# Inner loops in TensorE's program, and a first jump behind the unit loops, in a cached-attention decode kernel

## The chip, the cores and the metric

One core of a Trainium2 chip. The metric is the device time of one execution in microseconds (us). The kernel before was run three times: 1280.09 us in the median, 1279.94 to 1280.13.

## The reference: one decode step of attention and a gated layer

Four sequences (B), one new token each, 32 heads of 128, a cache of 8192 keys and values per head, all in bf16:

```python
h  = x + A(layernorm(x))
h2 = h + Bm(layernorm(h))
# A:  q = x @ wq, per head
#     p = softmax(einsum("bhqd,bhkd->bhqk", q, k_cache) * 128 ** -0.5)
#     A = einsum("bhqk,bhkd->bhqd", p, v_cache) @ wo
# Bm: (sigmoid(x @ w_gate) * (x @ w_up)) @ w_down
```

The two caches are 4 x 32 x 8192 x 128 elements each, 268 MB in bf16 each, and every element is used once. The weights (wq, wo, w_gate, w_up, w_down) make up some 14 MB more.

## The kernel before, in words

**Units.** The 128 pairs of sequence and head are taken four at a time: 32 units (`NU`). For one unit K is a load of 128 partitions by 64 KB (8.4 MB), and V another. Partition 32h + p holds 256 consecutive keys of head h.

**Slots and loads.** Three slots of 64 KB a partition lie in the tile KV: slots 0 and 1 for K of even and odd units, slot 2 for V (the last V goes to slot 0). SyncE (SP) issues all loads in one written-out order, wq first (L503), then k0, k1, v0, k2, v1, k3 and so on (L512). A K load waits until the transposes of the K in its slot are done (`t_kd`, a memset on VectorE, L342); a V load waits until the unit ahead of it has been weighted and summed (`t_vd`, the first product of L387). After the caches follow wo (L515) and w_gate (L517), w_up (L521), and three pieces of w_down (L526), each into a slot that came free. The output leaves by two small DMAs (L528).

**One unit** (`unit`). `k_chunk` runs 16 times: VectorE transposes 128 x 1024 words of K into one of two halves of kT (L327), and TensorE makes four products from it (L336), whose stationary operand is a window of the tile Lq, shifted by the number of the chunk. All 64 products of a unit sum into one PSUM bank, SBK; the first has `start`, the last `stop`. Then come the maxima (`maxima`, L343 to L348), the exponential on ScalarE (L350), the window of the next unit's query (`q_window`, L320), the weighting of V of the unit before (`pv`: 64 products of L377, the scaled copy L382 on ScalarE, four products of L387, which each run as two), and the transposed weights with their sum (`weights`, L356, L360).

**Order of work.** The class `_Prog` keeps one list of instructions for each engine, with the semaphore values that each waits for. `open`, `begin`, `end` and `close` turn a stretch that repeats into a hardware loop: the turns must be the same, and semaphores that belong to one engine are set back at each turn's end (`_rebase`, a semaphore instruction on L53). `play` (L110 to L118) writes the lists out; a loop's own edge has line L114. Unit 0 stands ahead of the loops. TensorE's loop has one unit a turn, 31 turns; that of VectorE and ScalarE has two units a turn, 15 turns, and the last unit stands behind it.

**Ends.** Ahead of the units, layer norm (L274 to L288), the query products from wq (L302) and their turning run. Behind them TensorE runs products that nobody reads, `filler` (L364: 36 ahead of the last `pv`, then 3, 10 and 4), the last `pv`, wo (L448), the second layer norm, gate and up (L467), down (L492), and VectorE adds the residual (L500).

Of the kernel before, what the change touches and what calls it, by code (L numbers as in the profile page):

```python
# [6 lines left out]
BF16 = mybir.dt.bfloat16  # L7
FP32 = mybir.dt.float32
ALU = mybir.AluOpType
ACT = mybir.ActivationFunctionType  # L10
AX = mybir.AxisListType


class _Prog:
    ENGS = ("sp", "act", "dve", "pool", "pe")

    def __init__(self, private):
        self.ops = {e: [] for e in self.ENGS}
# [4 lines left out]
        self.turn = {}  # L23
        self.turns = {}
        self.base = {}

    def token(self, key, by):
# [18 lines left out]
    def _rebase(self, eng):  # L46
        for key, owner in self.private.items():
            v = self.known[eng].get(key, 0)
            n = v - self.base.get(key, 0)
            if owner == eng and n:  # L50
                self.base[key] = v
                self._add(eng, ("rebase", key, n), lambda e, i, key=key, n=n:
                          e.wait_ge(self.sems[key], n).then_inc(self.sems[key], -n))  # L53

    def _add(self, eng, what, run):
        assert (eng in self.turn) == (eng in self.turns), eng
        if eng in self.turn:
            self.turn[eng].append((what, run))
        else:
            self.ops[eng].append(run)  # L60

    def _put(self, eng, todo, key, fn, incs, by):
        def run(e, i):
            for k, v in todo:
                e.wait_ge(self.sems[k], v)
            made = fn(e, i) if fn.__code__.co_argcount - len(fn.__defaults__ or ()) == 2 else fn(e)
# [6 lines left out]
        self._add(eng, (tuple(todo), key, incs), run)  # L73

    def emit(self, eng, fn, waits=(), incs=1, ch=None):
        todo = self._waits(eng, waits)
# [5 lines left out]
    def dma(self, eng, key, fn, waits=(), tok=None):  # L82
# [2 lines left out]
        self._put(eng, todo, key, fn, 1, 16)  # L85
        return tok

    def open(self, *engs):
        for e in engs:
            self._rebase(e)  # L90
            self.turns[e] = []

    def begin(self, *engs):
        for e in engs:
            self.turn[e] = []

    def end(self, *engs):
        for e in engs:
            self._rebase(e)
            self.turns[e].append(self.turn.pop(e))  # L100

    def close(self, *engs):
        for e in engs:
            first, *rest = self.turns.pop(e)
# [3 lines left out]
            self.ops[e].append((1 + len(rest), [m[1] for m in first]))  # L108

    def play(self, nc, name, e):  # L110
        for item in self.ops[name]:
            if isinstance(item, tuple):
                turns, runs = item
                with nc.Fori(0, turns, engines=OrderedEngineSet([e.engine])) as i:  # L114
                    for run in runs:
                        run(e, i)
            else:
                item(e, 0)  # L118


def bass_sequential_preLN__mha_block_cached__glu_gated_glu__decode_kernel(
# [13 lines left out]
    _, H, S, DH = A_k_cache.shape  # L135
# [6 lines left out]
    NU = B * H // HU  # L142
# [3 lines left out]
    TW = 1024  # L146
# [14 lines left out]
    with ExitStack() as es:  # L161
# [3 lines left out]
        def raw(t):  # L165
            return t.tensor if hasattr(t, "tensor") else t
# [146 lines left out]

        t_tr, t_sc, t_pv, t_ex, t_mx, t_exp, t_ptz, t_lq, t_ocp, t_rs, t_kd, t_vd, t_sum = ({} for _ in range(13))
        TU = 2

        def q_window(u, t=0):
            dst = bass.AP(raw(Lq), 15, [[528, 128], [128, 4], [16, 8]])
            msk = bass.AP(raw(mask), 0, [[8, 128], [0, 4], [1, 8]])
            t_lq[u] = emit("dve", lambda e, i: e.tensor_tensor(  # L320
                dst, bass.AP(raw(q_all), i * (4 * TU) + 4 * (u - TU * t), [[NU * 4, 128], [1, 4], [0, 8]]), msk, ALU.mult),
                           [t_q, t_lq0, t_mask, t_sc.get((u - 1, NT - 1))], ch="d2p")

        def k_chunk(u, c):
            o = slots["k", u] * (SLOT // 2) + c * TW
            w = [toks["k", u], t_sc.get((u, c - 2)) if c >= 2 else t_sc.get((u - 1, NT - 2 + c)), t_sum.get(u - 1) if c == 1 else None]
            t_tr[u, c] = emit("dve", lambda e: e.transpose(  # L327
                kT[:, (c % 2) * TW:(c % 2 + 1) * TW], KVw[:, o:o + TW]), w, ch="d2p")

            def f(e):  # L330
                ins = None
                for t in range(4):
                    hb, par = t // 2, t % 2
                    rhs = bass.AP(kTb.tensor, kTb.offset + (c % 2) * 2 * TW + hb * 64 + par,
                                  [[kTb.ap[0][0], 128], [128, 16], [2, 32]])
                    ins = e.matmul(bank[SBK], Lq[:, 128 * t + 15 - c:128 * t + 143 - c], rhs,  # L336
                                   start=(c == 0 and t == 0), stop=(c == NT - 1 and t == 3))
# [25 lines left out]
        def filler(n):  # L363
            emit("pe", lambda e: [e.matmul(bank[XS], Lq[:, 0:128], Lq[:, 0:512], start=True, stop=True) for _ in range(n)][-1],  # L364
                 [t_ps0, t_lq[NU - 1]], incs=0)

        def pv(u, t):
            t_rs[u] = emit("dve", lambda e: e.reciprocal(rsb[:, :], bank[QB[1]][:, 1:2]), [t_sum[u]], ch="d2a")  # L368
            slot = slots["v", u]
            ob = 512 * OBK  # L370

            def f(e, ks):
                made = []
                for k in ks:
                    j, n, r4 = k % 4, k // 4, k % 4
                    lhsT = PTz[:, 512 * r4 + n:512 * r4 + n + 481:32]
                    made.append(e.matmul(PS[32 * j:32 * j + 16, ob:ob + 512], lhsT,  # L377
                                         KV[:, slot * SLOT + 512 * k:slot * SLOT + 512 * (k + 1)],
                                         start=(k < 4), stop=(k >= 60), tile_position=(0, 32 * j)))
# [4 lines left out]
            def fs(e, i, qs):  # L384
                ins = None
                for q in qs:
                    ins = e.matmul(bass.AP(raw(PS), i * 4 + (512 * EX + 4 * (u - t)), [[4096, 128], [1, 4]]),  # L387
                                   O_sb[:, 128 * q:128 * (q + 1)], lane[:, q:q + 13:4],
                                   start=False, stop=(u == NU - 1 and q == 3), skip_group_check=True)
                return ins  # L390
            t_vd[u] = emit("pe", lambda e, i: fs(e, i, (0,)), [t_ocp[u], t_selc, t_ps0], ch="p2x")
            t_ex[u] = emit("pe", lambda e, i: fs(e, i, (1, 2, 3)), ch="p2d")

        def unit(u, t=0):
            for c in range(NT):
                k_chunk(u, c)
# [183 lines left out]
```

## Time and profile before

| what | value |
|---|---|
| median of three runs | 1280.09 us (1279.94 to 1280.13) |
| span of the profiled execution | 1278.5 us |
| the execution's own time beside the span | not recorded by itself; the median is 1.6 us longer than the span |
| instructions | 10886 |
| HBM read | 550.77 MB, 431 GB/s over the span |
| PE, DVE, ACT busy | 782.6, 759.6, 58.8 us |
| L336, the score products | x2048, 421 ns mean |
| L327, the transposes of K | x512, 1229 ns mean |

The span runs from the first to the last instruction of one profiled execution. PE is TensorE's products, PEld its weight loads, DVE VectorE, ACT ScalarE, POOL GpSimd, SP SyncE. "Busy" leaves out register, branch, semaphore and DMA-issuing instructions. [...]

### The profile page before, as it was taken

To read this page: it belongs to the slowest core of one execution; us is meant where nothing else is said; L and a number is where in the kernel's file an instruction comes from. 1 tells how busy PE (TensorE), PEld (TensorE's weight loads), DVE (VectorE), ACT (ScalarE), POOL (GpSimd) and SP (SyncE) were. 2 spreads that over 40 slices of the span, in tenths; PEclk is the share of its full clock that TensorE was granted. 3 is DMA by queue.
4 is the path that set the end of the run, shared out by engine and by line. 5 is a ranking of instruction groups with operands and counts; after the bars stand their busy time and mean duration, and the time that the engine had idled before them with its cause. 6 is when DMAs were issued, how large, how long until landed. Compare 5 with 4: busy or idle time off the path is not lost. (4 is left out here: it accounts for less than half of the span.)

```text
span 1278.5 us, 10886 instructions
## 1 busy us (share of the span) xinstructions
PE 782.6 (61%) x4609; PEld 292.2 (23%) x4609; DVE 759.6 (59%) x917; ACT 58.8 (5%) x114; POOL 5.7 (0%) x22
## 2 busy tenths in 40 slices
PE   1666765557755557755567655567655577555578
PEld 0222222222212222212222212222222222122223
DVE  1876765556665557665567655566655566655571
ACT  2000000000000000000000000000000000000001
POOL 1000000000000000000000000000000000000000
PEclk8888877788877788777788877788777888777889
DMA  9999999999999999999999999999999999999998
GB/s 425 425 427 431 437 443 426 431 429 445 435 429 429 435 443 431 429 431 439 441 426 431 429 445 435 429 429 435 443 431 429 431 441 439 426 431 429 443 437 343
DMA packets 10252, 550.83 MB, mean 431 GB/s; under 512 B 1148, under 2 KB 1160, under 8 KB 1416
## 3 DMA queue, kind: packets, MB, share of 16 engines
q1 hardware_dynamic: 10232, 550.77, 99.6%
q8 instruction: 3, 0.05, 0.0%
q10 hardware_dynamic: 16, 0.01, 0.0%
q14 instruction: 1, 0.01, 0.0%
HBM read 550.77 MB, written 0.00 MB: 431 GB/s over the span
## 5 line engine op out<-in xcount | busy, mean ns | idle before, releaser
L336 PE MATMUL PS<-kT,Lq 128*128 128x512 bf16 x2048 | 590.0, 421 | 347.2 <-DVE kT L327 329.5
L327 DVE STREAM_TRANSPOSE kT<-KV 128x1024 f32<-128x1024 f32 x512 | 611.7, 1229 | 307.9 <-DMA KV<-in_A_k_cache_dram 259.0
L336 PEld LDWEIGHTS PS<-kT,Lq 128*128 128x128 bf16 x2048 | 177.5, 104 | 746.7 <-DVE kT L327 581.4
L356 DVE STREAM_TRANSPOSE PTz<-E_sb 32x512 bf16<-32x512 bf16 x128 | 89.9, 703 | 128.9 <-PE PS L387 125.2
L377 PE MATMUL PS<-KV,PTz 128*16 128x512 bf16 x2048 | 116.9, 381 | 0.0
L360 PE MATMUL PS<-part,headw 128*128 128x2 f32 x64 | 17.8, 348 | 100.4 <-DVE PTz L356 100.4
L350 ACT ACTIVATE E_sb<-PS,negm 128x512 bf16<-128x512 f32 x32 | 22.0, 687 | 1141.3 <-DVE negm L348 1141.3
L377 PEld LDWEIGHTS PS<-KV,PTz 128*16 128x16 bf16 x2048 | 59.0, 110 | 56.0 <-issue 13.6
L387 PE MATMUL PS<-lane,kT 128*128 128x4 f32 x256 | 33.6, 255 | 30.8 <-ACT kT L382 30.8
L343 DVE TENSOR_REDUCE part<-PS 128x1 f32<-128x512 f32 x32 | 22.1, 692 | 35.9 <-PE PS L336 35.9
L387 PEld LDWEIGHTS PS<-lane,kT 128*128 128x128 f32 x256 | 31.0, 191 | 46.1 <-issue 44.7
L360 PEld LDWEIGHTS PS<-part,headw 128*128 128x128 f32 x64 | 15.1, 293 | 103.7 <-DVE PTz L356 103.7
L382 ACT ACTIVATE kT<-PS,rsb 128x512 f32<-128x512 f32 x32 | 22.0, 687 | 64.5 <-PE PS L377 64.5
L364 PE MATMUL PS<-Lq 128*128 128x512 bf16 x53 | 15.1, 447 | 0.1
L427 DVE TENSOR_TENSOR kT<-PS,mask 128x512 bf16<-128x512 f32 x1 | 0.7, 692 | 16.3 <-PE PS L387 16.3
L320 DVE TENSOR_TENSOR Lq<-q_all,mask 128x32 bf16<-128x32 bf16 x32 | 9.5, 298 | 0.0
L364 PEld LDWEIGHTS PS<-Lq 128*128 128x128 bf16 x53 | 5.6, 112 | 8.9 <-issue 5.3
L345 DVE STREAM_TRANSPOSE turn<-part 128x32 f32<-128x32 f32 x32 | 6.8, 212 | 1.1
L348 DVE STREAM_TRANSPOSE negm<-mxr 128x32 f32<-128x32 f32 x32 | 6.8, 211 | 1.1
L368 DVE RECIPROCAL rsb<-PS 128x1 f32<-128x1 f32 x32 | 6.3, 198 | 0.7 <-PE PS L360 0.7
L346 DVE TENSOR_SCALAR_CACHE_REDUCE turn<-turn 128x32 f32<-128x32 f32 x32 | 5.9, 186 | 1.1
L302 PE MATMUL PS<-KV,kT 128*4 128x512 bf16 x32 | 3.4, 594 | 5.1 <-DMA KV<-in_A_wq_dram 5.1
(65 smaller groups left out, 49.1 us busy)
## 6 DMA issues: line engine op xcount, KB each, us to landing
KV<-in_A_wq_dram SPq DMA_DIRECT2D x1, 4096.0 KB, 12.2
KV<-in_A_wo_dram SPq DMA_DIRECT2D x1, 4096.0 KB, 27.4
KV<-in_B_w_gate_dram SPq DMA_DIRECT2D x1, 1792.0 KB, 31.5
KV<-in_B_w_up_dram SPq DMA_DIRECT2D x1, 1792.0 KB, 35.3
KV<-in_B_w_down_dram SPq DMA_DIRECT2D x1, 1024.0 KB, 32.7
KV<-in_A_k_cache_dram SPq DMA_DIRECT2D x32, 50.3
KV<-in_A_v_cache_dram SPq DMA_DIRECT2D x32, 31.4
KV<-in_B_w_down_dram SPq DMA_DIRECT2D x1, 512.0 KB, 33.5
```

What stands on the lines that cost most here:

```text
L320: t_lq[u] = emit("dve", lambda e, i: e.tensor_tensor(dst, bass.AP(raw(q_all), i * (4 * TU) + 4 * (u - TU * t), [[NU * 4, 128], [1, 4], [0, ...
L327: t_tr[u, c] = emit("dve", lambda e: e.transpose(kT[:, (c % 2) * TW:(c % 2 + 1) * TW], KVw[:, o:o + TW]), w, ch="d2p")
L336: ins = e.matmul(bank[SBK], Lq[:, 128 * t + 15 - c:128 * t + 143 - c], rhs, start=(c == 0 and t == 0), stop=(c == NT - 1 and t == 3))
L343: a = emit("dve", lambda e: e.tensor_reduce(part[:, 0:1], bank[SBK], AX.X, ALU.max), [t_sc[u, NT - 1], t_pool], ch="d2d")
L345: a = emit("dve", lambda e: e.transpose(turn_[:, :], part[:, :]), [a], ch="d2d")
L350: t_exp[u] = emit("act", lambda e: e.activation(E_sb[:, :], bank[SBK], ACT.Exp, bias=negm[:, 0:1], scale=SCALE, accum_out=part[:, 1:2]), [ ...
L356: return [e.transpose(PTz[32 * q:32 * (q + 1), :].rearrange("p (r q c) -> p r q c", r=4, q=4)[:, :, q, :], E_sb[32 * q:32 * (q + 1), :].re ...
L360: t_sum[u] = emit("pe", lambda e: e.matmul(bank[QB[1]][:, 0:2], headw[:, :], part[:, 0:2], start=True, stop=True), [t_ptz[u], t_selc], ch= ...
L364: emit("pe", lambda e: [e.matmul(bank[XS], Lq[:, 0:128], Lq[:, 0:512], start=True, stop=True) for _ in range(n)][-1], [t_ps0, t_lq[NU - 1] ...
L377: made.append(e.matmul(PS[32 * j:32 * j + 16, ob:ob + 512], lhsT, KV[:, slot * SLOT + 512 * k:slot * SLOT + 512 * (k + 1)], start=(k < 4), ...
L382: t_ocp[u] = emit("act", lambda e: e.activation(O_sb, bank[OBK], ACT.Copy, scale=rsb[:, 0:1]), [t_pv[u], t_rs[u]], ch="a2p")
L387: ins = e.matmul(bass.AP(raw(PS), i * 4 + (512 * EX + 4 * (u - t)), [[4096, 128], [1, 4]]), O_sb[:, 128 * q:128 * (q + 1)], lane[:, q:q + ...
```

## The change

Three things are edited, and the class `_Prog` is extended to write nested loops.

First, the scores: a unit's 64 products become one clearing product with a weight tile of bf16 words and a moving operand of zeros (`clear`, with `start`), and a loop of 8 turns on TensorE. A turn holds two chunks; each product's window of Lq is addressed with the turn's number (`ix[-1] * 2`). For the window to move upwards with the turns, the chunks of K are read from the last to the first. VectorE's 16 transposes stay written out.

Second, the products that nobody reads: 36 become 12 turns of 2, and 10 become 5 turns of 2.

Third, on TensorE and VectorE the program from its beginning to the end of its unit loop is put in a loop of two turns with a condition (`second`, `done`): in turn 0 the engine jumps over all of it to the code behind, in turn 1 it runs it.

```diff
+    def second(self, eng):
+        self.outer[eng].append(self.list[eng])
+        self.list[eng] = []
+
+    def done(self, eng):
+        made, self.list[eng] = self.list[eng], self.outer[eng].pop()
+        self.list[eng].append((("second", [m[0] for m in made]), _Second(made)))
...
+                if isinstance(run, _Loop):
+                    with nc.Fori(0, run.turns, engines=OrderedEngineSet([e.engine])) as i:
+                        go(run.items, ix + [i])
+                elif isinstance(run, _Second):
+                    with nc.Fori(0, 2, engines=OrderedEngineSet([e.engine])) as i:
+                        with e.If_ne(e.to_reg(i), 0):
+                            go(run.items, ix)
...
+        prog.second("pe")
+        prog.second("dve")
...
+        headb = headw[:, :].bitcast(BF16)[:, 0:128]
+        zeros = bass.AP(raw(Lq), 0, [[528, 128], [0, 512]])
...
+        def clear(bk, waits=()):
+            emit("pe", lambda e: e.matmul(bank[bk], headb, zeros, start=True, stop=False, skip_group_check=True),
+                 waits, incs=0)
...
-            o = slots["k", u] * (SLOT // 2) + c * TW
+            o = slots["k", u] * (SLOT // 2) + (NT - 1 - c) * TW
...
-                    ins = e.matmul(bank[SBK], Lq[:, 128 * t + 15 - c:128 * t + 143 - c], rhs,
-                                   start=(c == 0 and t == 0), stop=(c == NT - 1 and t == 3))
+                    ins = e.matmul(bank[SBK], bass.AP(raw(Lq), ix[-1] * 2 + (128 * t + c % 2), [[528, 128], [1, 128]]), rhs,
+                                   start=False, stop=False, skip_group_check=True)
...
-            t_sc[u, c] = emit("pe", f, [t_tr[u, c], t_lq[u]], ch="p2d")
+            t_sc[u, c] = emit("pe", f, [t_tr[u, c]], ch="p2d")
+
+        def scores(u):
+            clear(SBK, [t_lq[u], t_pool, t_ps0, t_selc])
+            prog.open("pe")
+            for c in range(NT):
+                if c % 2 == 0:
+                    prog.begin("pe")
+                k_chunk(u, c)
+                if c % 2:
+                    prog.end("pe")
+            prog.close("pe")
...
             if u == NU - 1:
                 prog.close("dve", "act")
+                prog.done("dve")
                 t = 0
...
         prog.close("pe")
-        filler(36)
+        prog.done("pe")
+        filler(2, 12)
...
-        filler(10)
+        filler(2, 5)
```

More of the change, by code (lines that the diff above doesn't have):

```diff
@@ L11, with __init__ @@
 AX = mybir.AxisListType
+class _Loop:
+    def __init__(self, turns, items):
+        self.turns, self.items = turns, items
+class _Second:
+    def __init__(self, items):
+        self.items = items
 class _Prog:
@@ L17, in __init__ @@
     def __init__(self, private):
-        self.ops = {e: [] for e in self.ENGS}
+        self.list = {e: [] for e in self.ENGS}
+        self.outer = {e: [] for e in self.ENGS}
         self.sems = {}
@@ L22, in __init__ @@
         self.private = private
-        self.turn = {}
-        self.turns = {}
         self.base = {}
@@ L51, in _rebase, with run @@
                 self.base[key] = v
[L52 to L60, printed above, removed]
+                self.list[eng].append((("rebase", key, n), lambda e, ix, key=key, n=n:
+                                       e.wait_ge(self.sems[key], n).then_inc(self.sems[key], -n)))
     def _put(self, eng, todo, key, fn, incs, by):
-        def run(e, i):
+        def run(e, ix):
             for k, v in todo:
                 e.wait_ge(self.sems[k], v)
-            made = fn(e, i) if fn.__code__.co_argcount - len(fn.__defaults__ or ()) == 2 else fn(e)
+            made = fn(e, ix) if fn.__code__.co_argcount - len(fn.__defaults__ or ()) == 2 else fn(e)
             made = made if isinstance(made, list) else [made]
@@ L71, in run @@
                     m.then_inc(self.sems[key], by)
-        self._add(eng, (tuple(todo), key, incs), run)
+        self.list[eng].append(((tuple(todo), key, incs), run))
     def emit(self, eng, fn, waits=(), incs=1, ch=None):
@@ L90, in open @@
             self._rebase(e)
-            self.turns[e] = []
+            self.outer[e].append((self.list[e], []))
     def begin(self, *engs):
         for e in engs:
-            self.turn[e] = []
+            self.list[e] = []
     def end(self, *engs):
@@ L99, in end @@
             self._rebase(e)
-            self.turns[e].append(self.turn.pop(e))
+            self.outer[e][-1][1].append(self.list[e])
+            self.list[e] = None
     def close(self, *engs):
         for e in engs:
-            first, *rest = self.turns.pop(e)
+            self.list[e], (first, *rest) = self.outer[e].pop()
             for t, made in enumerate(rest):
@@ L107, in close, with go @@
                 assert not d and len(made) == len(first), (e, t + 1, d[:4])
-            self.ops[e].append((1 + len(rest), [m[1] for m in first]))
+            self.list[e].append((("loop", 1 + len(rest), [m[0] for m in first]), _Loop(1 + len(rest), first)))
     def play(self, nc, name, e):
[L111 to L118, printed above, removed]
+        def go(items, ix):
+            for _, run in items:
+                if isinstance(run, _Loop):
[5 more added lines that the diff above has]
+                            go(run.items, ix)
+                else:
+                    run(e, ix)
+        go(self.list[name], [])
 def bass_sequential_preLN__mha_block_cached__glu_gated_glu__decode_kernel(
@@ L315, in bass_sequential_preLN__mha_block_cached__glu_gated_glu__decode_kernel, with at @@
         TU = 2
+        headb = headw[:, :].bitcast(BF16)[:, 0:128]
+        zeros = bass.AP(raw(Lq), 0, [[528, 128], [0, 512]])
+        def at(ix, d):
+            return ix[d] if len(ix) > d else 0
+        def clear(bk, waits=()):
+            emit("pe", lambda e: e.matmul(bank[bk], headb, zeros, start=True, stop=False, skip_group_check=True),
+                 waits, incs=0)
         def q_window(u, t=0):
@@ L328, in k_chunk, with f @@
                 kT[:, (c % 2) * TW:(c % 2 + 1) * TW], KVw[:, o:o + TW]), w, ch="d2p")
-            def f(e):
+            def f(e, ix):
                 ins = None
@@ L361, in weights, with filler @@
                             [t_ptz[u], t_selc], ch="p2d")
-        def filler(n):
-            emit("pe", lambda e: [e.matmul(bank[XS], Lq[:, 0:128], Lq[:, 0:512], start=True, stop=True) for _ in range(n)][-1],
-                 [t_ps0, t_lq[NU - 1]], incs=0)
+        def filler(n, turns=1):
+            if turns > 1:
+                prog.open("pe")
+            for _ in range(turns):
+                if turns > 1:
+                    prog.begin("pe")
+                emit("pe", lambda e: [e.matmul(bank[XS], Lq[:, 0:128], Lq[:, 0:512], start=True, stop=True) for _ in range(n)][-1],
+                     [t_ps0, t_lq[NU - 1]], incs=0)
+                if turns > 1:
+                    prog.end("pe")
+            if turns > 1:
+                prog.close("pe")
         def pv(u, t):
@@ L382, in pv, with fs @@
             t_ocp[u] = emit("act", lambda e: e.activation(O_sb, bank[OBK], ACT.Copy, scale=rsb[:, 0:1]), [t_pv[u], t_rs[u]], ch="a2p")
-            def fs(e, i, qs):
+            def fs(e, ix, qs):
                 ins = None
                 for q in qs:
-                    ins = e.matmul(bass.AP(raw(PS), i * 4 + (512 * EX + 4 * (u - t)), [[4096, 128], [1, 4]]),
+                    ins = e.matmul(bass.AP(raw(PS), at(ix, 0) * 4 + (512 * EX + 4 * (u - t)), [[4096, 128], [1, 4]]),
                                    O_sb[:, 128 * q:128 * (q + 1)], lane[:, q:q + 13:4],
@@ L390, in fs @@
                 return ins
-            t_vd[u] = emit("pe", lambda e, i: fs(e, i, (0,)), [t_ocp[u], t_selc, t_ps0], ch="p2x")
-            t_ex[u] = emit("pe", lambda e, i: fs(e, i, (1, 2, 3)), ch="p2d")
+            t_vd[u] = emit("pe", lambda e, ix: fs(e, ix, (0,)), [t_ocp[u], t_selc, t_ps0], ch="p2x")
+            t_ex[u] = emit("pe", lambda e, ix: fs(e, ix, (1, 2, 3)), ch="p2d")
         def unit(u, t=0):
-            for c in range(NT):
-                k_chunk(u, c)
+            scores(u)
             maxima(u)
```

4 lines of the change are left out of this document (2 added, 2 removed).

## The prediction, made before the changed kernel ran

> **What bounds the kernel now.** I read the page's busy times and DMA queues first, because they say whether any engine could be the limit at all.
>
> ```profile
> span 1278.5 us, 10886 instructions
> ...
> PE 782.6 (61%) x4609; PEld 292.2 (23%) x4609; DVE 759.6 (59%) x917; ACT 58.8 (5%) x114; POOL 5.7 (0%) x22
> ...
> q1 hardware_dynamic: 10232, 550.77, 99.6%
> q8 instruction: 3, 0.05, 0.0%
> ...
> q14 instruction: 1, 0.01, 0.0%
> ```
>
> No compute engine is above 61%, while the packets of the data queue fill 99.6% of sixteen engines' span. There are also four packets of program code, three of 16 KB (0.05 MB over 3) and one smaller. Next come the stages, to see whether the transfers ever pause and what happens at both ends (columns: length, busy time of PE, PEld, DVE, ACT, POOL with counts, granted clock, DMA share, GB/s).
>
> ```profile
> 0.00:1.50 1.50, 0.00 (x0) 0.00 (x0) 0.00 (x0) 0.09 (x1) 0.61 (x9) 1.00 0.00 0
> ...
> 500.00:1200.00 700.00, 428.99 (x2547) 160.93 (x2548) 423.91 (x511) 27.16 (x56) 0.00 (x0) 0.81 1.00 434
> ...
> 1273.00:1274.00 1.00, 0.37 (x2) 0.00 (x0) 0.94 (x3) 0.00 (x0) 0.00 (x0) 1.00 0.59 229
> 1274.00:1275.00 1.00, 0.95 (x16) 0.65 (x16) 0.15 (x1) 0.00 (x0) 0.00 (x0) 1.00 0.21 84
> 1275.00:1276.00 1.00, 0.86 (x14) 0.36 (x12) 0.00 (x0) 0.00 (x0) 0.00 (x0) 1.00 0.03 12
> ```
>
> For 700 us the sixteen DMA engines are full at 434 GB/s, that is 27.1 GB/s each. The stream starts after 1.5 us and thins out from 1273: the last three windows hold 0.59 + 0.21 + 0.03 = 0.83 us of mean engine time, yet stretch towards 1276. If all engines ended together, they would end at 1273.8. So **the end waits for a few late DMA engines**. The chain of work that ended last shows who waits:
>
> ```profile
> 1241.63 33.54 DMA KV<-in_B_w_down_dram
> ...
> 1275.21 0.60 PE PS L492 x8
> ...
> 1275.83 0.43 PE PS L492 x4
> ...
> 1276.29 0.42 DVE KV L500
> ```
>
> The last two pieces of w_down release the last down products at 1275.21 and 1275.83; the add and the output follow, 1278.5 − 1275.8 = 2.7 us. The 33.54 us are queueing behind earlier loads, no latency that an earlier issue would shorten. Evenly finished engines would gain at most 1275.8 − 1273.8 = 2.0 us. That is the ceiling for anything that leaves the 550.77 MB alone, as this change does.
>
> **Where code loading costs time.** The DMA view, asked for four short windows (2, 2, 3 and 3 us), places the four code packets; its last column is a share of sixteen engines.
>
> ```profile
> q8 instruction: 1, 0.02, 3.1%
> ```
>
> ```profile
> q14 instruction: 1, 0.01, 1.0%
> ```
>
> ```profile
> q8 instruction: 1, 0.02, 2.2%
> ```
>
> ```profile
> q8 instruction: 1, 0.02, 2.3%
> ```
>
> They lie in 53 to 55, 60 to 62, 84 to 87 and 1261 to 1264 us. Their durations: 3.1% x 16 x 2 = 1.0 us, 1.0% x 32 = 0.3, 2.2% x 48 = 1.1, 2.3% x 48 = 1.1. One packet holds up one DMA engine, and as every engine is full, that engine stays late to the end. By bytes alone 16 KB cost 0.6 us (16.4 KB over 27.1 GB/s); if the interrupted data packet also pays, both together are 1.7. I take 1.1 to 1.5. One such delay on top of an ordinary spread of some tenths explains most of the 2.0 us.
>
> The three q8 packets follow TensorE's place in its code: the end of unit 0, the end of the first unit turn, and the tail. From the first to the second lie about 128 matmuls with their loads, some 260 instructions. The other 30 turns, which jump back over the same code, fetched nothing. The q14 packet fits VectorE as it enters its loop. I read this as blocks of about 260 instructions, each fetched when the block ahead of it is entered and then kept.
>
> **The change, part by part.** *Jump behind and back.* Each of the two engines passes once to the code behind its unit loops before its first work. Counted in the code, TensorE has 469 matmuls before (38 ahead of unit 0, 66 in it, 138 in the loop body, 227 behind) and 330 after, hence about 970 and 700 instructions. By the same blocks, the code behind the new loops lies in the second block; touching it fetches the third block at the start instead of at 84 us. The packet at 53 us should thus go to about 2 us, the one at 84 to the tail, the one at 1262 should vanish, and VectorE's go from 60 us to the start.
>
> ```profile
> 0.80 0.41 SPq L503 DMA_DIRECT2D KV<-in_A_wq_dram  x1
> ...
> 13.09 3.35 PE L302 MATMUL PS<-KV,kT 128*4 128x512 bf16 x32 [5.13 <-DMA KV<-in_A_wq_dram]
> ```
>
> But wq is issued at 0.80, and packets flow from 1.5 to 2 us. A fetch that TensorE triggers after its own start, near 1 us, meets that stream or just precedes it: it costs its DMA engine 0 to 1.5 us. It stalls nothing else, because wq's products start only at 13.09 us. The one left in the tail costs 1.1 to 1.5 on some engine, as the old ones did. So the last engine is late by about one fetch, as before: −0.7 to +0.2 us; I take **−0.3**, since fewer engines are hit and the tail's may fall on an early one.
>
> [...]
>
> *Inner loops for the scores.* Sixteen chunks of four matmuls become eight turns of two. Each turn adds a loop edge, a semaphore correction and up to eight computed weight addresses. The old steady state:
>
> ```profile
> 1180.34 15.53 DVE L327 STREAM_TRANSPOSE kT<-KV 128x1024 f32<-128x1024 f32 x13 [0.30 <-PE PS L336]
> ...
> 1193.55 2.19 PE L336 MATMUL PS<-kT,Lq 128*128 128x512 bf16 x8 [0.20 <-DVE kT L327]
> ```
>
> VectorE sets the pace, 15.53 / 13 = 1.19 us a chunk, 2.39 for two; TensorE needs 2.19 and waits 0.20. The nearest rows for the additions come from the chain: VectorE's own loop edge, and the gap after L382 before a product whose address is computed.
>
> ```profile
> 1203.36 0.04 DVEq L114
> ...
> 1203.49 0.65 issue
> ...
> 1240.71 0.14 issue
> ```
>
> An edge costs at most 0.04 + 0.65 = 0.69 us, an address at most 0.14; all exposed, 0.69 + 8 x 0.14 = 1.81 a turn; all hidden, 0. Shorter turns are excluded, since VectorE's transposes stay. I take 0.3, because the sequencer can prepare while a chunk's matmuls (about 1 us) run, and only a chunk's first address follows its wait. That is 8 x 0.3 = 2.4 us a unit, on the path from K's landing to the next V issue. Its cover:
>
> ```profile
> 1163.42 0.33 SPq L512 DMA_DIRECT2D KV<-in_A_v_cache_dram  x1
> ...
> 1201.93 0.81 SPq L512 DMA_DIRECT2D KV<-in_A_v_cache_dram  x2
> ...
> 1214.26 2.37 DVE L327 STREAM_TRANSPOSE kT<-KV 128x1024 f32<-128x1024 f32 x2 [8.68 <-DMA KV<-in_A_k_cache_dram]
> ```
>
> SP issues V 30 at 1201.93, and its turn in the queue comes when K 31 has landed, at 1214.2: 12.3 us early, less about 1 us from issue to first packet (0.80 to 1.5 and later). So a unit may lengthen by **11 us**, or 1.4 us a turn, before DMA starves. 2.4 cost nothing.
>
> *The clearing product* opens the sum: one 128x512 matmul, 0.2 to 0.4 us (rows below), while TensorE waits for the next K (8.68 above). Its wait for the query window and the pool's constants stands where the first chunk waited before; behind it is only that unit's work. *Reading K's chunks in reverse* changes no duration and waits for the same landing.
>
> *Fillers.* 36 become 12 turns of 2, and 10 become 5 turns of 2.
>
> ```profile
> 1246.00:1252.00 6.00, 6.00 (x16) 2.21 (x15) 0.00 (x0) 0.00 (x0) 0.00 (x0) 0.53 0.87 377
> 1252.00:1256.50 4.50, 4.50 (x25) 1.87 (x23) 0.00 (x0) 0.00 (x0) 0.00 (x0) 1.00 0.95 408
> ...
> 1245.66 10.90 PE L364 MATMUL PS<-Lq 128*128 128x512 bf16 x36
> ...
> 1256.49 3.65 PE L377 MATMUL PS<-KV,PTz 128*16 128x512 bf16 x64
> ...
> 1270.30 0.93 PE L467 MATMUL PS<-KV,kT 128*4 128x448 bf16 x16 [0.27 <-DVE kT L288]
> ...
> 1271.47 0.93 PE L467 MATMUL PS<-KV,kT 128*4 128x448 bf16 x16 [0.24 <-DMA KV<-in_B_w_up_dram]
> ...
> 1274.05 2.17 PE L492 MATMUL PS<-KV 128*4 128x256 bf16 x28 [0.68 <-DMA KV<-in_B_w_down_dram]
> ```
>
> In the first window 16 take 6.0 us at a clock of 0.53 (0.38 each), the 20 or so left take 4.5 (0.22 each). Twelve fewer save 12 x 0.22 = 2.6 us; gaps at turns of up to 0.69 give some back, and a score path longer by 2.4 starts them later. The last unit's products thus begin at 1256.5 give or take 2. Work there is late by little: the up products wait 0.24 for their weights, the down products 0.68. At an unchanged clock I cost this at 0.
>
> **Sum.** 1278.5 − 0.3 + 0 + 0 = 1278.2 of span. The median is 1280.09, 1.6 over the profiled span, for what lies around it; so 1278.2 + 1.6 = **1279.8**.
>
> **The rivals.**
> *All code packets leave the stream* (the tail fetches nothing, and the start's precede wq): of the 2.0 us one fetch of 1.3 goes and an ordinary spread of 0.7 stays, so 1280.1 − 1.3 = 1278.8. For it: the code shrinks by a block. Against it: 700 instructions and the program's end still pass a third block's start.
> *Nothing moves*: the jump loads nothing early or each fetch returns later: 1280.1.
> *Fetches or edges at every turn (slower).* If a turn exceeds 1.4 us of added time, V's issue comes late and each unit starves DMA. At the full 1.81 that is 8 x 0.41 = 3.3 us a unit, times 31 = 102: 1382. A branch that fetches (1.1 a packet, besides 0.69 of edge) gives the same 1.8. Against it: 30 unit turns without a packet, and addresses that hide behind matmuls.
> *A cold tail*: the sparser fillers leave the granted clock at 0.5. Gate, up and down products double: 0.93 + 0.93 + 2.0 = +3.9 of work, less about 0.24 + 0.68 of waiting and what of down's work lies between landings (0.8 or more): about +1.5, so 1281.3, up to 1282 without that last. [...]
>
> **How the numbers follow.** Forecast 0.55 (1279.8, own range 1279.2 to 1280.3), packets gone 0.18 (1278.8), nothing moves 0.12, cold tail 0.10 (1281.3), starving 0.05. The range 1278.7 to 1281.4 takes in all but starving and the ends of the two outer cases. Faster by over 0.2% (2.56 us, about what a measurement can tell from no change; below 1277.5) would beat the 2.0 us ceiling: 0.02. Slower by over 0.2%: starving 0.05 and 0.02 from the cold tail. Within: 0.91.
>
> **What would show it.** Code packets on q8 near 2 us and near 1260, none between; the share of q1 still above 99%; windows from 1273 that still thin out over some 2 us; VectorE still waiting for K in each unit, by 2 to 3 us less. Wrong would be: no code packet in the tail (gain of 1.3), q8 packets by the hundred or idle DMA between 100 and 1200 us (starving), or a clock of 0.5 after 1262.

## The result: slower by 0.15%, above the predicted range

The changed kernel took 1282.11 us in the median of 21 runs (1280.39 to 1284.21), the kernel before, run beside it, 1280.06 in the median of 21 (1279.88 to 1281.11). The ratio is 1.0015, with a 95% interval of 1.001 to 1.0021. The forecast was 1279.8 with a range up to 1281.4. The direction of the forecast was wrong by its sign, and a second thing changed that it did not look for: of the kernel before, 19 of the 21 runs lie within half a microsecond (two are at 1281.1), while those of the changed kernel lie over nearly 4 us.

The profiled execution of the changed kernel took 1282.4 us, of which 1280.7 are span. From its page, the lines that answer to those shown of before:

```profile
span 1280.7 us, 14086 instructions
...
PE 802.9 (63%) x4629; PEld 327.9 (26%) x4629; DVE 762.5 (60%) x917; ACT 58.7 (5%) x114; POOL 5.7 (0%) x22
...
q1 hardware_dynamic: 10232, 550.77, 99.5%
q8 instruction: 2, 0.03, 0.0%
```

The data queue is still full, and there are 2 packets of TensorE's code where there were 3. The DMA view places them, first for 4 to 6 us, then for 1260 to 1262 us:

```profile
q8 instruction: 1, 0.02, 3.6%
...
q14 instruction: 1, 0.01, 1.0%
```

```profile
q8 instruction: 1, 0.02, 3.5%
```

So both engines' packets moved to the start, where they come at about 5 us, and one of TensorE's stays in the tail. What the jump was to do to code loading, it does. The time went two other ways.

**The data come 1 us later.** The timeline of the changed kernel (start, duration, engine, line, what it waited for) along the first units and at two later K's:

```profile
14.51 3.58 PE L319 MATMUL PS<-KV,kT 128*4 128x512 bf16 x32 [6.56 <-DMA KV<-in_A_wq_dram]
...
61.45 2.37 DVE L353 STREAM_TRANSPOSE kT<-KV 128x1024 f32<-128x1024 f32 x2
...
66.47 16.04 DVE L353 STREAM_TRANSPOSE kT<-KV 128x1024 f32<-128x1024 f32 x13 [0.46 <-PE PS L362]
...
88.67 0.33 SPq L559 DMA_DIRECT2D KV<-in_A_v_cache_dram  x1
...
131.34 2.37 DVE L353 STREAM_TRANSPOSE kT<-KV 128x1024 f32<-128x1024 f32 x2 [8.12 <-DMA KV<-in_A_k_cache_dram]
...
1215.20 2.37 DVE L353 STREAM_TRANSPOSE kT<-KV 128x1024 f32<-128x1024 f32 x2 [7.47 <-DMA KV<-in_A_k_cache_dram]
```

The same places in the kernel before, as far as they were not shown:

```profile
58.89 2.37 DVE L327 STREAM_TRANSPOSE kT<-KV 128x1024 f32<-128x1024 f32 x2
...
85.42 0.33 SPq L512 DMA_DIRECT2D KV<-in_A_v_cache_dram  x1
...
130.60 2.37 DVE L327 STREAM_TRANSPOSE kT<-KV 128x1024 f32<-128x1024 f32 x2 [8.25 <-DMA KV<-in_A_k_cache_dram]
```

wq's products start at 14.51, 1.4 later than the 13.09 of before. Thirteen transposes take 16.04 against 15.53. Together SP issues V 1 at 88.67, 3.25 later than before. The reader should notice that unit 1 starts its transposes (58.89, 61.45) without any wait for DMA: its K has long been there, and units 0 and 1 run back to back. From K 3 on, every unit waits for its K, and that K lands 0.74 later (131.34 against 130.60), at K 31 0.94 later. The windows from 80 to 100 us show the place; first before, then after (a packet counts in the window where it starts, so the drop shows that a round of packets slipped, not its exact price):

```profile
80.00:100.00 20.00, 12.02 (x95) 5.37 (x93) 10.87 (x17) 1.47 (x3) 0.00 (x0) 0.74 1.04 450
```

```profile
80.00:100.00 20.00, 14.76 (x105) 6.50 (x104) 13.04 (x21) 1.47 (x3) 0.00 (x0) 0.83 0.96 403
```

450 GB/s became 403: there the load queue ran dry for a moment.

**The tail runs at half clock.** The timeline of TensorE and of the final add in the changed kernel:

```profile
1254.61 3.65 PE L423 MATMUL PS<-KV,PTz 128*16 128x512 bf16 x64
...
1263.92 3.59 PE L495 MATMUL PS<-KV,kT 128*4 128x512 bf16 x32 [2.03 <-DMA KV<-in_A_wo_dram]
...
1268.29 1.86 PE L500 MATMUL PS<-kT,lane 128*4 128x512 f32 x2 [0.78 <-ACT kT L499]
...
1276.67 1.69 PE L539 MATMUL PS<-KV 128*4 128x256 bf16 x28
...
1278.43 0.42 DVE L547 TENSOR_TENSOR KV<-PS,kT 36x256 bf16<-36x256 f32 x1 [1.10 <-PE PS L539]
```

The windows of the same stretch, with the granted clock ahead of the DMA share:

```profile
1274.00:1275.00 1.00, 1.00 (x24) 0.48 (x20) 0.00 (x0) 0.05 (x1) 0.00 (x0) 1.00 0.85 328
1275.00:1276.00 1.00, 1.00 (x18) 0.35 (x8) 0.22 (x1) 0.49 (x1) 0.00 (x0) 1.00 0.18 72
1276.00:1277.00 1.00, 0.88 (x11) 0.32 (x11) 0.93 (x4) 0.00 (x0) 0.00 (x0) 1.00 0.03 12
...
1254.00:1261.50 7.50, 5.85 (x82) 3.25 (x80) 0.92 (x2) 2.17 (x3) 0.00 (x0) 1.00 0.98 422
1262.00:1272.00 10.00, 7.30 (x39) 1.77 (x40) 1.38 (x4) 1.46 (x3) 0.00 (x0) 0.50 0.98 415
1272.20:1278.00 5.80, 5.41 (x72) 2.58 (x72) 1.89 (x6) 1.89 (x5) 0.00 (x0) 1.00 0.49 198
```

In the kernel before, wo's products ran at full clock:

```profile
1263.71 1.90 PE L448 MATMUL PS<-KV,kT 128*4 128x512 bf16 x32
```

With fewer fillers the last unit's products are done at 1258.3 instead of 1260.1, TensorE then waits 2.03 us for wo, and for about 10 us from 1262 the clock is 0.50. wo's products take 3.59 instead of 1.90. The DMA stream thins out about 1 us later than before (0.85, 0.18, 0.03 against 0.59, 0.21, 0.03 one window earlier), but the down products no longer wait for it: they start at 1276.67 (1274.05 before) and run through without a pause, and the final add starts 2.1 us later (1278.43 against 1276.29). The chain of work that ended last runs from wo's landing through TensorE, and no DMA stands behind these lines in it:

```profile
1236.31 27.56 DMA KV<-in_A_wo_dram
...
1263.92 3.69 PE PS L495 x32
...
1276.67 1.74 PE PS L539 x28
```

Had the clock stayed up, the data alone would have cost about 1 us (an estimate: the last windows with DMA come about 1 us later).

### The profile page after: what moved, and what is told of

Same layout as the page of the kernel before. It is cut to its first block, busy times and chain, and to the rows that moved or that the text cites. A ratio compares the mean times of both kernels' runs of the same rounds, so it can differ in the third digit from the quotient of the medians.

```text
span 1280.7 us, 14086 instructions
## 1 busy us (share of the span) xinstructions
PE 802.9 (63%) x4629; PEld 327.9 (26%) x4629; DVE 762.5 (60%) x917; ACT 58.7 (5%) x114; POOL 5.7 (0%) x22
## 3 DMA queue, kind: packets, MB, share of 16 engines
q1 hardware_dynamic: 10232, 550.77, 99.5%
## 4 chain that ended last, share of the span: by engine, by line
DMA 53%; PE 18%; DVE 11%; issue 2%; ACT 1%; another core or an unknown queue 1%; SPq 0%; DVEq 0%
DMA KV<-in_A_k_cache_dram 50%; PE PS L362 13%; DVE kT L353 10%; PE PS L423 4%; DMA KV<-in_A_wo_dram 2%; ACT kT L428 1%; PE PS L433 0%; SPq L559 0%; PE PS L495 0%; PE PS L406 0%; PE PS L500 0%; PE PS L514 0%; PE PS L539 0%; DVE PTz L393 0%
## 5 line engine op out<-in xcount | busy, mean ns | idle before, releaser
L362 PEld LDWEIGHTS PS<-kT,Lq 128*128 x2048 | 210.9, 103 | 695.6 <-issue 623.3
L340 PE MATMUL PS<-Lq,headw 128*128 128x512 bf16 x32 | 18.8, 587 | 10.8 <-issue 9.5
```

The lines of the kernel that those rows point to most:

```text
L340: emit("pe", lambda e: e.matmul(bank[bk], headb, zeros, start=True, stop=False, skip_group_check=True), waits, incs=0)
L362: ins = e.matmul(bank[SBK], bass.AP(raw(Lq), ix[-1] * 2 + (128 * t + c % 2), [[528, 128], [1, 128]]), rhs, start=False, stop=False, skip_g ...
```

## The experiments

Two theories had to be told apart. **A, the late stream:** the jump's code packet holds up wq, the inner loops lengthen units 0 and 1, V 1 goes out too late, and the load queue runs dry near 89 us. **B, the cold tail:** fewer products that nobody reads let TensorE wait for wo, and the clock falls. The rival of both was that one of the three edits makes all of it by itself. Each kernel was run 11 times beside 26 to 33 runs of the kernel before. I compare spans, since in a few executions, of the kernel before too, the time around the span is about 1 us longer (1281.23 with a span of 1278.3). The kernel before has spans of 1278.1 to 1278.8 with a mean of 1278.38 (one of 92 lies at 1280.2).

### The changed kernel without the jump

```diff
-        prog.second("pe")
-        prog.second("dve")
...
-                prog.done("dve")
...
-        prog.done("pe")
```

> The changed kernel without the first jump: inner loops and looped fillers stay. Theory A (late stream): the code packets at 5 us hold up wq by 1.4 us, so V 1 is issued at 88.7 instead of about 87.2 and the load queue runs dry near 89 us; without the jump wq lands near 13.0, the score products start near 33.8, V 1 goes out at 87.2 plus or minus 0.5, no dry spot, the last data land about 1 us earlier than in the changed kernel. Theory B (cold tail): the sparser fillers leave the clock at one half from 1262, and the jump has nothing to do with it: still 1281 to 1282.2 and a cold tail. A alone: 1280.1. Both at work: 1281.0 with a span whose part after the last landing stays near 3.9 us.

Median 1280.18, ratio 1.0005 (0.9996 to 1.0014). The spans form two groups: six from 1278.1 to 1278.4, five from 1279.8 to 1280.3, with a mean of 1279.11. The profiled execution, 1278.1, shows V 1's issue and wo's products:

```profile
86.71 0.33 SPq L555 DMA_DIRECT2D KV<-in_A_v_cache_dram  x1
```

```profile
1262.56 3.42 PE L491 MATMUL PS<-KV,kT 128*4 128x512 bf16 x32 [0.96 <-DMA KV<-in_A_wo_dram]
...
1266.76 1.02 PE L496 MATMUL PS<-kT,lane 128*4 128x512 f32 x2 [0.79 <-ACT kT L495]
```

No dry spot, as A had it. The clock falls even here, though in this execution for a short time only: wo's products take 3.42, the two after them 1.02 as in the kernel before (1.86 at half clock, above). The end was not moved. This execution is of the lower group; none of the upper group was profiled. That the upper group has a longer cold tail is argued from the clocks of all executions, under the table of the eight combinations. If so, B needs no jump.

### The changed kernel with the old fillers

```diff
-        filler(2, 12)
+        filler(36)
...
-        filler(2, 5)
+        filler(10)
```

> The changed kernel with the fillers written out again (36 and 10 products): jump and inner loops stay. Theory B (cold tail): the clock stays at 1.0 through the tail in every run, the part after the last landing is back at 2.7 us, and the spread of the runs (1280.4 to 1284.2) shrinks to some tenths. Theory A (late stream): the dry spot near 89 us stays, with 1.0 us of the excess: 1281.1. A alone: 1282.1 with the spread as it is; B alone: 1280.1.

Median 1281.14, ratio 1.0003 (0.9994 to 1.0012). Spans from 1278.2 to 1279.8, mean 1278.99. In the profiled execution (1279.7):

```profile
88.50 0.33 SPq L559 DMA_DIRECT2D KV<-in_A_v_cache_dram  x1
```

```profile
1264.50 1.90 PE L495 MATMUL PS<-KV,kT 128*4 128x512 bf16 x32
```

The clock is up again, and what is left is the late stream, 0.6 us in the mean and up to 1.4. The spread did not shrink to tenths as B expected: the late stream has a spread of its own.

### The jump alone, and the looped fillers alone

The first is the kernel before with `second` and `done`, the second the kernel before with `filler(2, 12)` and `filler(2, 5)`.

> The kernel before with the first jump as its only edit (scores and fillers written out). Theory A: wq lands 1.4 us late, V 1 goes out near 86.9 instead of 85.4, which is still ahead of the end of K 2 near 89.4, so no dry spot: 1280.1 plus or minus 0.4. If the late wq alone makes the stream late (the rival within A), 1281. Theory B: 1280.1, since the fillers are the old ones.

> The kernel before with the looped fillers (12 turns of 2, 5 turns of 2) as its only edit. Theory B: the last unit's products start some 2 us earlier, TensorE then waits for wo, the clock falls to one half near 1262 in at least some executions: 1281 to 1282, with a spread of more than 1 us. Theory A: 1280.1 with the spread of the kernel before (0.2 us).

The jump alone: median 1280.23, ratio 1.0 (0.9991 to 1.0009), mean span 1278.50, one of eleven at 1279.7, the others 1278.2 to 1278.6. Its wq is as late as in the changed kernel, but V 1 is not late enough:

```profile
14.53 3.58 PE L319 MATMUL PS<-KV,kT 128*4 128x512 bf16 x32 [6.57 <-DMA KV<-in_A_wq_dram]
```

```profile
87.50 0.33 SPq L552 DMA_DIRECT2D KV<-in_A_v_cache_dram  x1
```

A late wq cost nothing by itself in ten of eleven executions. The fillers alone: median 1280.26, ratio 1.0002 (0.9993 to 1.0011), seven spans from 1278.2 to 1278.6 and four from 1279.2 to 1279.7, mean 1278.80. Two groups, as B expected, though the upper one cost 1 us and not up to 2, and its median is that of the kernel before.

### The inner loops alone

```diff
+            clear(SBK, [t_lq[u], t_pool, t_ps0, t_selc])
+            prog.open("pe")
...
+            prog.close("pe")
```

(the chunks in reverse order and the computed weight addresses go with it)

> The kernel before with the inner score loops as its only edit (no first jump, fillers written out). Theory A (the queue runs dry when V 1 is issued later than about 88 us, which takes the late wq of the jump and the longer units together): V 1 goes out near 86.9, no dry spot, spans 1278.2 to 1278.6 as in the kernel before. Rival: the inner loops alone make the stream late: spans of 1279 and above in most executions.

Median 1280.10, ratio 0.9998 (0.9989 to 1.0007), spans 1278.1 to 1278.9, mean 1278.38, the same as before.

```profile
86.82 0.33 SPq L555 DMA_DIRECT2D KV<-in_A_v_cache_dram  x1
```

```profile
80.00:100.00 20.00, 13.78 (x99) 5.94 (x98) 11.43 (x19) 1.47 (x3) 0.00 (x0) 0.74 1.04 450
```

The loops' additional instructions (its page counts 14055 in place of 10886) cost nothing alone.

### Unit 0 late, and nothing else

```diff
+            for _ in range(3 if (u, c) == (0, 0) else 0):
+                w = w + [emit("dve", lambda e: e.transpose(kT[:, 0:TW], KVw[:, o:o + TW]), w, ch="d2d")]
```

> The kernel before with three more transposes of the first K chunk in unit 0 alone, about 1.2 to 1.3 us each; the output is the same. No jump, no loops, old fillers: only V 1 moves, from 85.4 to about 89.2 us. Theory A: the queue runs dry near 89 us and the spans go to 1279 to 1280, though a single early delay of 3.8 us is the only edit. Rival (the later units have 11 us of cover and absorb it): spans of 1278.2 to 1278.7.

Median 1282.39, ratio 1.0016 (1.0007 to 1.0025). All eleven spans lie above 1279.6, mean 1280.55: as slow as the changed kernel, from some 5 us added once, at the start of a run of 1278 (3.8 us and spans of 1279 to 1280 were expected). The profiled execution (1280.7) shows V 1's issue, the dry spot and, in the tail, wo's products:

```profile
90.39 0.33 SPq L514 DMA_DIRECT2D KV<-in_A_v_cache_dram  x1
```

```profile
80.00:100.00 20.00, 14.59 (x105) 6.08 (x103) 13.29 (x20) 1.46 (x3) 0.00 (x0) 0.86 0.96 401
```

```profile
1265.06 3.53 PE L450 MATMUL PS<-KV,kT 128*4 128x512 bf16 x32 [1.25 <-DMA KV<-in_A_wo_dram]
```

This is theory A alone, without jump, loops or fewer fillers. With all 36 fillers, a late wo lets TensorE wait 1.25 us here, and its products run at 3.53: late data can cool the tail. But that is not what this execution lost its time by. The chain that ended last goes back to a piece of w_down that landed at 1277.34, against 1275.16 in the kernel before:

```profile
1242.05 35.29 DMA KV<-in_B_w_down_dram
...
1277.38 0.60 PE PS L494 x8
```

The data alone are 2.2 us late, which is all of the excess.

### 36 in loops, and 24 written out

The first is the changed kernel with `filler(2, 18)`, the second the kernel before with `filler(24)`.

> The changed kernel with 18 turns of 2 ahead of the last unit's products, so 36 in loops in place of 24. Theory B as refined (their number sets when the last unit's products run, and the wait for wo behind them lets the clock fall; that they stand in a loop is harmless): clock of 1.0 through the tail, spans as with the fillers written out, 1278.2 to 1279.8. If the loop's gaps are what lets the clock fall: spans of 1280 to 1282 as in the changed kernel.

> The kernel before with 24 products in place of 36, written out, as its only edit. [...] If the loop is what matters: all near 1278.4.

36 in loops: median 1281.27, ratio 1.0007 (0.9998 to 1.0016), spans 1278.5 to 1280.3, mean 1279.35, which is near the written-out fillers' 1278.99 and 1.15 below the changed kernel (the upper end lies above the 1279.8 that was expected); in its profile TensorE is at full clock:

```profile
1264.28 1.90 PE L495 MATMUL PS<-KV,kT 128*4 128x512 bf16 x32
```

24 written out: median 1281.08, ratio 1.0004 (0.9995 to 1.0013), five spans from 1278.2 to 1278.7 and six from 1279.3 to 1279.8:

```profile
1245.47 7.54 PE L364 MATMUL PS<-Lq 128*128 128x512 bf16 x24
...
1263.02 3.59 PE L448 MATMUL PS<-KV,kT 128*4 128x512 bf16 x32 [2.17 <-DMA KV<-in_A_wo_dram]
```

It is their number, not the loop: the two groups are there without a loop. The last unit's products follow the fillers at once, are done sooner, and the wait for wo grows to 2.17 us. The profiled execution, 1278.7, is of the lower group, and its cold wo products cost the end at most some tenths.

### The jump on one engine only

Both are the inner loops with written-out fillers; the first has `second` on TensorE alone, the second on VectorE alone.

> Inner loops and written-out fillers, with the first jump on TensorE alone. If its 16 KB packet at about 5 us is what holds up wq: wq's last piece lands near 14.2 as with both jumps (13.0 without), V 1 goes out near 88.5, the queue runs dry, spans from 1278.2 to 1279.8 with a mean near 1279.0. If VectorE's 8 KB packet is the one: wq near 13.0 to 13.3, V 1 near 87, spans of 1278.4.

> Inner loops and written-out fillers, with the first jump on VectorE alone. If TensorE's 16 KB packet is what holds up wq: wq near 13.0 to 13.8 (8 KB cost about 0.9 us on one engine, which need not be the last), V 1 near 87, no dry spot, spans of 1278.4 plus or minus 0.2. If VectorE's packet is enough: wq above 14, V 1 near 88.5 and spans up to 1279.8.

TensorE alone: median 1281.56, ratio 1.001 (1.0001 to 1.0019), ten of eleven spans from 1279.4 to 1280.4, mean 1279.63. VectorE alone: median 1280.20, ratio 1.0002 (0.9993 to 1.0011), ten of eleven from 1278.1 to 1278.7, one of 1280.5, mean 1278.55. wq's products, V 1's issue and the window, first TensorE, then VectorE:

```profile
14.25 3.58 PE L318 MATMUL PS<-KV,kT 128*4 128x512 bf16 x32 [6.29 <-DMA KV<-in_A_wq_dram]
...
88.23 0.33 SPq L557 DMA_DIRECT2D KV<-in_A_v_cache_dram  x1
...
80.00:100.00 20.00, 14.61 (x106) 6.60 (x105) 13.06 (x20) 1.47 (x3) 0.00 (x0) 0.83 0.96 396
```

```profile
13.79 3.46 PE L318 MATMUL PS<-KV,kT 128*4 128x512 bf16 x32 [5.85 <-DMA KV<-in_A_wq_dram]
...
87.36 0.33 SPq L557 DMA_DIRECT2D KV<-in_A_v_cache_dram  x1
...
80.00:100.00 20.00, 14.06 (x103) 6.36 (x103) 12.75 (x19) 1.47 (x3) 0.00 (x0) 0.83 1.05 453
```

TensorE's packet makes the difference: 88.23 is dry, 87.36 is not. VectorE's packet holds up wq too, by 0.7 us (the 0.9 on one engine that I expected was an estimate), and that is still covered. That TensorE's jump alone is slower than both jumps together (1279.63 against 1278.99, and against the 1279.0 that was expected) is not explained. The profile with VectorE's jump has wo's products at half clock, though all 36 fillers run and the wait is short:

```profile
1262.64 3.42 PE L493 MATMUL PS<-KV,kT 128*4 128x512 bf16 x32 [0.17 <-DMA KV<-in_A_wo_dram]
```

Its span is 1278.3: cold wo products by themselves cost nothing.

### The jump and the looped fillers, without inner loops

> The first jump and the looped fillers on written-out scores, the last of the eight combinations. Theory A: V 1 goes out near 87.5 as with the jump alone, no dry spot in most executions. Theory B: the two groups of the looped fillers alone, near 1278.4 and near 1279.5. Together a mean span of 1278.8 to 1279.2; if the jump and the fillers made the excess without the loops, 1280 and more.

Median 1280.24, ratio 1.0005 (0.9996 to 1.0014), mean span 1279.05: six spans from 1278.2 to 1278.5, five from 1279.1 to 1281.2. Its V 1 goes out at 86.97. It looks like the fillers' effect, with one execution at 1281.2 that is longer than any with the fillers alone.

### All eight combinations

| edits | mean span, us | over before |
|---|---|---|
| none | 1278.38 | |
| inner loops | 1278.38 | 0.0 |
| jump | 1278.50 | 0.1 |
| looped fillers | 1278.80 | 0.4 |
| jump and inner loops | 1278.99 | 0.6 |
| jump and looped fillers | 1279.05 | 0.7 |
| inner loops and looped fillers | 1279.11 | 0.7 |
| all three (the change) | 1280.50 | 2.1 |

Only one of the 21 spans of the changed kernel lies below 1279. A mean of eleven is uncertain by 0.1 to 0.3 (the spread of the spans over the root of their number), so that the rows from 0.4 to 0.7 are not told apart. The three edits' single effects add up to 0.5. The rest, 1.6, is their joint effect: the jump and the inner loops together starve the queue once, and with fewer fillers a long cold tail comes on top in some executions.

That the longer executions have a longer cold tail was seen in one of them only, the profiled one of the changed kernel. The mean granted clock is known for every execution and bears it out for others. Ten us at half clock lower a mean over 1280 us by 0.004 (0.5 x 10.2 / 1280, an estimate). The kernel before has means of 0.814 to 0.816 or, at a second level, of 0.821 to 0.824, and one of 0.812. Without the jump, the six short executions have 0.814, and the five long ones 0.811, 0.812 or, at the second level, 0.820. With jump and looped fillers the short ones have 0.814 or 0.822, the long ones 0.813 or 0.820. In the changed kernel the twelve executions with 0.811, 0.812 or 0.820 span 1280.3 to 1282.5, the nine others 1278.7 to 1280.3; the means are 1281.1 and 1279.7. By this the late stream alone costs it some 1.3 us, and the executions with a long cold tail, about half, take 1.5 more. It is not excluded that data which come later still are a part of these 1.5, since a longer wait for wo also cools the tail (1.25 us with a late unit 0). In the three kernels that issue V 1 at 88.2 to 88.7 and have 36 fillers ahead of the last unit's products (old fillers, 36 looped, TensorE's jump alone) all 33 means are 0.816 to 0.817 or 0.823 to 0.824, with spans from 1278.2 to 1280.4: that spread is the stream's own.

## Why the prediction was wrong, by its steps

*What bounds the kernel* stood: the data queue at 99.5%, and the last DMA engines set the stream's end. The ceiling of 2.0 us on a gain was never tried.

*Code packets.* Where they would go was right but for the time: to the start, though at 5 us and not at 2, and one near 1260, with one packet fewer. (By the prediction's own way of counting, the changed code holds 317 matmuls, not 330; nothing hangs on it.) That code comes in blocks of some 260 instructions was my reading of where the packets lie; the runs show the packets, not the blocks. The step that failed is **"It stalls nothing else, because wq's products start only at 13.09 us"**. Those products start when all of wq has landed, and the packet sits in the middle of that load: 14.51. The step weighed the packet against the engine's idle time and not against the transfer that ends the idle time. The delay of 1.1 to 1.5 us that I priced at the stream's end is the same delay on the first load: 1.4.

*Inner loops.* The term was 0.3 us a turn, an estimate between 0 and 1.81; measured it is (16.04 − 15.53) / 6.5 = 0.08, so addresses and loop edges hide almost fully here. The step that failed is **"So a unit may lengthen by 11 us"**. I read the cover at unit 30 and took it for all units. At unit 30 it was right: the changed kernel's units grew, and from K 5 (0.93 late) to K 31 (0.94) no K came later for it. But units 0 and 1 run back to back behind the first loads, and there the cover of V 1 ends near 88 us: issues at 86.7, 86.8, 87.4 and 87.5 ran no dry spot, those at 88.2, 88.5, 88.7 and 90.4 did. Against 85.42 that is some 2.6 us, not 11, and less in other executions: the kernel with 24 fillers, whose code is the same up to there, issued V 1 at 86.23. The change moved the issue by 3.25: 1.4 from wq, some 1.3 from two longer units (2 x 8 x 0.08), and the rest is no more than such a difference between executions. My rival "starving" named the mechanism, but asked 1.4 us a turn of it, at every unit; it needed one unit, once.

*Fillers.* "At an unchanged clock I cost this at 0" held only with its condition. The fillers took 7.55 us against 10.90, 3.4 less where I had 2.6, and the last unit's products started at 1254.6, in the range that I gave. What followed is the rival called a cold tail, with 0.10 and +1.5, though by another way: it was to come from sparse fillers, while here the clock was up through the last unit's products and fell after them. The sign that I had named for it, a clock of 0.5 after 1262, came. That the size fits is luck: it was added up from gate, up and down products, which in the changed profile ran at full clock from 1273.89; at half clock ran wo's products (3.59 against 1.90) and the two behind them (1.86 against 1.02). By the clocks above, a cost of it is there in about half of the executions: 1.7 us in five of eleven without the jump, about 1 us with the fillers alone, 1.5 in twelve of 21 of the changed kernel. The clock itself was the missing step: TensorE's work between the last unit and wo is light (a wait of 2 us, 1.05 us of small products), and I never asked what the clock would do there.

In six profiles TensorE waits for wo, by 0.17 to 2.2 us, and wo's products take 3.42 to 3.59 us; in six it does not wait, and they take 1.90. From the end of the last unit's products to wo's products there are 3.8 to 6.1 us in the first six and 3.6 in the others. In the changed kernel the clock is 0.50 from 1261.87 to 1272.11, which is 10.24 us, read in windows of 0.1 us. In the other five that wait, the two products behind wo's take 1.02 again and not 1.86, so the clock was up by then; with 24 fillers written out it is 0.50 from 1260.5 to 1266.5 and 1.00 from 1267. The four of these five with data in time have spans of 1278.1 to 1278.7, so that only the long half clock was seen to set the end. Why the same kernel falls into two groups of executions no run shows.

*The sum.* Forecast: −0.3 + 0 + 0. Measured in the profiled execution: about +1.0 from the stream, and about 1.1 more from the tail, together 2.2 of span. Both were rivals or near them, each held to be unlikely; that both can come in one execution was not considered, and so the range ended 0.7 us too low.

**What stays open.** Why a dry spot costs 0 in some executions and 1.4 us in others with the same kernel (jump and inner loops: 1278.2 to 1279.8). That it hangs on which DMA engine the code packet meets is a guess and was not tried. In the kernel with a late unit 0, K 31 landed 0.88 late and the last pieces of w_down some 2.2; why the two differ was not looked into. Why the clock is up again at the products behind wo's in five profiles, and in the changed kernel only after 10.2 us, is open. Single late executions (1281.2 with jump and fillers, 1280.5 with VectorE's jump, 1279.7 with the jump alone, 1280.2 of the kernel before) have no trace; their mean clocks (0.820, 0.821, 0.815 and 0.812, the last the lowest of 92) lie 0.001 to 0.004 below one of the two levels of their kernels (0.822, 0.824, 0.816 and 0.816). A longer cold tail fits them, no more than that. No kernel here beats the kernel before; the inner loops alone equal it.

## What to carry to other kernels

Cover must be read where it is smallest, and in a pipeline that is its first turns, before the steady waits have formed: here some 2 to 2.6 us at unit 1 against 11 at unit 30, and 5 us lost there once cost as much as the whole change. One packet of code was a delay for the load that it fell into: put at the start, it fell into the load on which everything waits and cost that load 1.2 to 1.6 us. Work that nobody reads can be part of the schedule: 24 fillers in place of 36 moved the idle gap to the next wait (2.03 us for wo in the changed kernel, then 10.2 us at a clock of 0.50), and the price came out in only some of the executions, so that the profiles of the kernels with fewer fillers and data in time, all of shorter executions, did not show it. The mean granted clocks of all executions hint at it.

## What the runs showed of the hardware that was not expected

One packet of 16 KB of code, at about 5 us in the changed kernel, moved the start of wq's products by more than the 1.1 us that it lasted: by 1.2 us with TensorE's jump alone (14.25 against 13.09 before), by 1.2 to 1.6 with both jumps (14.29 to 14.69). VectorE's smaller packet, 0.3 us long, moved it by 0.7 (13.79). Without a jump, with inner loops and looped fillers, the start is 13.06.

A load queue that ran dry for a moment near 89 us left the later loads late to the end of the run (0.74 us at K 3, 0.93 at K 5, 0.94 at K 31): the queue is full from then on, and nothing was caught up.

The granted clock stayed at 0.50 for 10.24 us in the changed kernel's tail, although TensorE was busy for 7.3 of the 10 us from 1262. In the profiles of the kernel before and of the changed one, read in windows of 0.1 us up to 1278, all 66 stretches below full clock last 6.83, 10.24, 13.65 or 17.07 us, whole multiples of 3.41.
